# Steps between the matmuls of a one-core attention and feed-forward block: features inside the last queries' matmuls, output weights and row steps with free steps between, memory steps one by one as their buffers need

## The chip, the core and the metric

The kernel runs on one core of a Trainium2 chip, in one launch. The metric is the device time of that launch in microseconds, lower is better. The engines of the core run side by side, each through its own queue in order: TensorE (PE in the profile) multiplies, VectorE (DVE), ScalarE (ACT) and GpSimd (POOL) work element by element, and SyncE (SP) issues most of the transfers; ScalarE issues some too. An instruction that waits holds up everything behind it on its engine.

## The reference, cut to what matters

```
x: 2048 rows of 512;  mod = silu(c) @ w_mod  ->  sa, ca, ga, sb, cb, gb
h  = layernorm(x) * (1 + ca) + sa
q, k, v = h @ wq, h @ wk, h @ wv          # 32 heads of 16, 4 segments of 512 rows
for each segment s:
    a_dot = softmax(q k^T / 4 + causal mask) v          # inside the segment
    a_mem = phi(q) M / (phi(q) z + 1e-6)                # phi(t) = t + 1 if t > 0 else exp(t)
    o     = g * a_mem + (1 - g) * a_dot                 # g = sigmoid(beta), one for each head
    M, z += phi(k)^T v, sum of phi(k)
x  = x + ga * (o @ wo)
h  = layernorm(x) * (1 + cb) + sb
x  = x + gb * (((h @ w_gate) * (h @ w_up)) @ w_down)    # hidden size 1376
```

Data are float32. The kernel keeps float32 accuracy with products of high and low halves: a matrix `a` becomes `aH` (a copy in a shorter format, made by ScalarE) and `aL = a - aH` (made by VectorE or GpSimd), and a product takes three matmuls, H x H, L x H and H x L.

## The kernel before

**Attention loop.** The heads are worked through in 32 units `u` of four heads each: unit `u` belongs to segment `u // 8` and group `u // 2 % 4` of eight heads. The main loop runs over `v` from -2 to 32, with five slots each. In slot `i` of turn `v` TensorE computes logits for the row maxima of a unit one or two ahead (`q_step`: tiles `q`, reduced by VectorE into `nm`), does what `fill` gives it, and then the logits of unit `v` (`k_step`: tile `k`, turned by ScalarE into `pt` with one Exp, masked by GpSimd). Once per turn 16 products with the values (`av_step`, tile `tb`) are put in. There is one buffer for `k`, so the `k_step` of a slot waits until ScalarE has read the one before. The maxima of a unit go through a transpose (`ntp`, `nt`) and by DMA into two extra rows of its queries (`n_step`). I call "row v.i" what TensorE does from the `k_step` of slot i in turn v to the next `k_step`.

**Fill.** All other work of the block is cut into steps by two generators, `fill_a` (attention: row statistics and features `a_ln`, projections `a_kq` and `a_v`, memory steps `a_mem`, conditioning `a_mod`) and `fill_b` (output projection `wo_mm`, second layer norm `lnC`, first steps of the feed-forward part). A step yields its cost on TensorE; `fill` takes steps until the slot's credit is used up. `yield 0.0` costs nothing, `yield False` ends the slot's filling, `yield None` means that nothing can be done yet. `weave(a, b, at)` runs `a` and puts one step of `b` behind each place of `a` that `at` names.

**Features.** `a_ln(s + 1)` makes, for the next segment, row statistics (four steps), the reciprocal deviation (ScalarE, then five small operations on GpSimd), four scalings of rows on VectorE, and then for each of four column blocks d a transpose (`atp`), a scaled copy (`ahf`, ScalarE), `ahH` (ScalarE) and `ahL` (GpSimd). The first projection of the next segment, `kps{s+1}_0`, reads `ahH` and `ahL` of all four blocks, one after the other.

**Memory steps.** `a_mem(s, g)` transposes phi(k) (`mp`, copied to `pkr`), multiplies phi(q) with the memory in two halves (`up`, copied to `us`) and updates the memory (`mz`); one PSUM buffer (`sm`) serves them all. `memq` holds the waiting generators; `drain` runs all of them before the phi of a query projection is allocated. phi tiles rotate through three buffers.

**After the loop** comes the feed-forward part: 22 weight preparations (`prep`, each loading `w_gate` and `w_up` columns by four DMAs and splitting them into halves `AH`, `AL`), products `g`, and the down projection `acc`.

**What sets the order.** A scheduler places the instructions of each engine; matmuls are chained in program order, and `pin` ties an instruction behind the last matmul issued before it. An instruction that is not pinned can be placed earlier. Eight semaphores serve all DMAs in turn, so a DMA can be issued only once the DMA eight before it has landed.

## Time and profile before

| what | value |
|---|---|
| time, median of 3 runs | 881.3 us (879.98 to 881.94) |
| the profiled execution, its own time | 881.91 us |
| its span, first to last instruction | 879.8 us |
| mean granted TensorE clock | 0.992 |
| busy: TensorE, VectorE, ScalarE, GpSimd | 832.8, 650.6, 472.5, 424.1 us |
| attention loop, first to last `k_step` | 59.1 to 516.1 us of the span |

A line of the timeline gives start, length, engine, source line, operation, tiles (out<-in, buffer numbers left out), shape and count, and in brackets how long the engine had been idle before it and what ended that. L90 is the helper through which every matmul goes, L40 one through which VectorE's operations go, so the tile names tell the place.

### The profile page before, as it was taken

The numbers are of one execution on the slowest core, as the hardware profiler recorded it, in microseconds if no ns is written. First come the engines' busy times: TensorE is split into PE (matmuls) and PEld (weight loads), VectorE is DVE, ScalarE is ACT, GpSimd is POOL, SyncE is SP. The second block draws the span as 40 slices with busy tenths as digits, with TensorE's granted clock in tenths as the row PEclk, the third lists the DMA queues.
The fourth block names the chain that finished last, engine by engine and source line by source line (L and its number), as shares of the span: only waits on it lengthen the run. The fifth ranks groups of instructions, "written<-read, shape, count | busy, mean of one in ns | idle before, by whom it ended". The sixth has DMA issues, their size and how long they took to land.

```text
span 879.8 us, 14406 instructions
## 1 busy us (share of the span) xinstructions
PE 832.8 (95%) x4824; PEld 583.0 (66%) x4824; DVE 650.6 (74%) x1728; ACT 472.5 (54%) x740; POOL 424.1 (48%) x564
## 2 busy tenths in 40 slices
PE   8998999989999989999978899999999999999998
PEld 5765565555565656655644567788778888887886
DVE  7697677986778868788888759898784856666532
ACT  3757667777677766777554664333363523333321
POOL 4545546546455665486352533987200846550000
PEclk9999899999999999999999999999999999999999
DMA  7774456665648665677695552543414232212032
GB/s 236 225 235 159 146 160 201 214 209 174 207 142 252 199 190 157 220 234 239 209 285 177 160 180 97 176 146 105 163 30 127 87 120 64 56 55 93 0 118 96
DMA packets 112667, 139.46 MB, mean 159 GB/s; under 512 B 20112, under 2 KB 71312, under 8 KB 112592
## 3 DMA queue, kind: packets, MB, share of 16 engines
q1 hardware_dynamic: 106368, 130.91, 48.7%
q10 hardware_dynamic: 6224, 7.62, 2.4%
q8 instruction: 38, 0.62, 0.3%
q14 instruction: 37, 0.30, 0.1%
HBM read 87.48 MB, written 50.76 MB: 157 GB/s over the span
## 4 chain that ended last, share of the span: by engine, by line
PE 66%; DVE 13%; DMA 8%; ACT 5%; POOL 4%; issue 3%; ACTq 1%; SPq 0%; POOLq 0%; DVEq 0%
PE g L90 23%; PE acc L90 14%; PE tb L90 5%; DVE q L40 5%; PE k L90 5%; PE q L90 5%; PE vps L90 4%; PE kps L90 3%; PE qps L90 2%; ACT pt L330 2%; DMA xr<-in_x_dram 2%; PE wops L90 2%; POOL ahL L223 1%; DVE x L40 1%; DVE nm L40 1%
## 5 line engine op out<-in xcount | busy, mean ns | idle before, releaser
L40 DVE CUSTOM_DVE_ANT_0 q<-q,cmask 128x384 f32<-128x384 f32 (+3 forms) x512 | 246.7, 508 | 66.4 <-PE q L90 56.4
L330 ACT ACTIVATE pt<-k 128x1024 f32<-128x1024 f32 x160 | 163.8, 1024 | 68.7 <-PE k L90 47.3
L333 POOL TENSOR_SCALAR_AFFINE_SELECT pt<-pt 128x256 f32<-128x256 f32 (+1 forms) x224 | 105.4, 484 | 174.3 <-ACT pt L330 173.9
L90 PE MATMUL q<-kst,qst 96*128 96x384 bf16 (+3 forms) x512 | 102.1, 301 | 11.7 <-DVE nm L40 10.4
L90 PE MATMUL k<-qst,kst 98*128 98x384 bf16 (+3 forms) x512 | 97.9, 303 | 11.6 <-ACT pt L330 10.7
L448 POOL TENSOR_TENSOR w<-w 128x256 f32<-128x256 f32 (+1 forms) x84 | 72.0, 869 | 55.7 <-DMA w<-in_w_up_dram 38.2
L443 POOL TENSOR_TENSOR AL<-w,AH 128x512 fp32r<-128x512 f32 (+1 forms) x42 | 58.2, 1388 | 48.0 <-ACT AH L439 46.8
L90 PE MATMUL tb<-pt,v 128*32 128x512 f32 (+3 forms) x1024 | 76.2, 438 | 0.2 <-POOL pt L333 0.2
L90 PEld LDWEIGHTS <-kst 98*128 98x128 bf16 x512 | 38.8, 99 | 56.6 <-issue 48.4
L40 DVE DVE_READ_ACCUMULATOR2_ANT nm<- 128x1 f32 x512 | 72.3, 141 | 0.0
L90 PEld LDWEIGHTS <-qst 96*128 96x128 bf16 x512 | 43.6, 98 | 39.1 <-issue 14.4
L439 ACT ACTIVATE AH<-w 128x512 fp32r<-128x512 f32 (+3 forms) x88 | 46.8, 565 | 33.6 <-POOL w L448 20.5
L1453 DVE TENSOR_TENSOR mL<-mid,mH 128x512 fp32r<-128x512 f32 (+1 forms) x44 | 32.9, 751 | 41.4 <-ACT mH L1452 39.4
L90 PE MATMUL acc<-DH,mL 128*128 128x512 f32 x144 | 56.6, 393 | 0.9 <-DVE mL L1453 0.9
L90 PE MATMUL acc<-DH,mH 128*128 128x512 f32 x144 | 57.2, 397 | 0.0
L90 PE MATMUL acc<-DL,mH 128*128 128x512 f32 x144 | 56.5, 393 | 0.0
L90 PEld LDWEIGHTS tb<-pt,v 128*32 128x32 f32 x1024 | 28.7, 110 | 39.5 <-issue 35.9
L1452 ACT ACTIVATE mH<-mid 128x512 fp32r<-128x512 f32 (+1 forms) x44 | 27.1, 627 | 51.7 <-PE acc L90 50.1
L1245 ACT ACTIVATE p<-g 128x512 f32<-128x512 f32 (+1 forms) x22 | 13.1, 597 | 73.2 <-PE g L90 73.1
L443 DVE TENSOR_TENSOR AL<-w,AH 128x512 fp32r<-128x512 f32 (+3 forms) x44 | 29.2, 671 | 19.1 <-ACT AH L439 18.2
L359 ACT ACTIVATE tsb<-tb 128x512 f32<-128x512 f32 x32 | 19.1, 596 | 35.0 <-PE tb L90 33.4
L90 PE MATMUL g<-chH,AH 128*128 128x512 f32 (+1 forms) x88 | 34.8, 395 | 0.7 <-ACT p L1245 0.7
(286 smaller groups left out, 2060.1 us busy)
## 6 DMA issues: line engine op xcount, KB each, us to landing
kst<-kd SPq DMA_DIRECT2D x32, 384.0 KB
qst<-qd SPq DMA_DIRECT2D x32, 384.0 KB
td<-tsb ACTq DMA_DIRECT2D x28, 256.0 KB
wm<-in_w_mod_dram SPq DMA_DIRECT2D x24, 256.0 KB
kd<-k SPq DMA_DIRECT2D x16, 384.0 KB
qd<-q SPq DMA_DIRECT2D x16, 384.0 KB
w<-in_w_gate_dram SPq DMA_DIRECT2D x40, 128.0 KB
w<-in_w_up_dram SPq DMA_DIRECT2D x40, 128.0 KB
```

Of the source, the lines that this page charges most:

```text
L40: i = getattr(self.eng, name)(*a, **k)
L90: return pe(nc.tensor.matmul(*a, **k))
L223: nc.gpsimd.tensor_sub(lo, h, hi.bitcast(F32))
L330: lpt[0] = act.activation(pt, kp, AF.Exp, scale=0.25)
L333: sels[u, i] = nc.gpsimd.affine_select(w, w, pattern=[[0, w.shape[1]], [1, P]], compare_op=ALU.is_ge, fill=0.0, base=0, channel_multiplier=-1)
L359: act.activation(tsbs[u], tbs.pop(u), AF.Copy)
L439: i = act.activation(hi[sl], w[sl], AF.Copy)
L443: i = eng.tensor_sub(lo[sl], w[sl], hi[sl].bitcast(F32))
L448: i = ce.tensor_tensor(w[:, o, :, 0:n], w[:, x, :, 0:n], w[:, y, :, 0:n], op=op)
L1245: lcp[0] = act.activation(r["p1"], ps, AF.Copy)
L1452: pin(act.activation(mH[0:n], md[0:n], AF.Copy))
L1453: vec.tensor_sub(mL[0:n], md[0:n], mH[0:n].bitcast(F32))
```

## The change

1. Features: the slot-ending steps between column blocks now stand only in the second layer norm, and `a_ln` is woven so that the four blocks of the next segment come out inside the last query projection (`qps{s}_3`) instead of behind it.
2. Memory steps: `drain` is gone. Before a phi tile is allocated, memory steps run only while the user of the tile three before it is not done (for the last segment: all, as before). The VectorE operation that ends phi (`later`) waits one more slot unless someone asks for it.
3. Output weights: all four tiles of `wo` are loaded at once into the buffers of the rows, and scaling, high half and low half of a tile stand in three different steps; the two first residual tiles take the buffers that the weights had. In `wo_op` the high half is pinned too, and the low half is made one step later.
4. Row steps of the second layer norm, and the first weight preparation (`prep(0, ...)`), take other places between the products of the output projection: the preparation moves from beside `wo_mm(1)` to beside `wo_mm(2)`.
5. DMAs: the two row transfers of `n_step` become one (32 fewer on ScalarE's queue), the four loads of a weight preparation three (22 fewer on SyncE's).

```diff
@@ -226,7 +226,7 @@
             if kept_h is not None:
                 kept_h.append(h)
             yield 0.45
-            if not first and d % 2 == 1:
+            if pfx == "c" and d % 2 == 1:
                 yield False
         return hH, hL
 
@@ -306,8 +306,7 @@
         TP(tp, nms.pop(u).rearrange("p a b -> p (a b)"), identb)
-        for i in range(2):
-            nc.scalar.dma_start(Q[96 + i:97 + i].rearrange("p h (q t) -> p (h q) t", t=P), nt[16 * i:16 * i + 16])
+        nc.scalar.dma_start(Q[96:98].rearrange("p h (q t) -> p (h q) t", t=P), nt)
 
     def k_step(u, i):
 
@@ -428,8 +427,9 @@
 
         f0, n = ft[i]
         w = rpool.tile([P, 8, 2, P], F32, tag="W", name=f"w{key}", bufs=rb)
-        for src, k0, j in ((w_gate, 0, 0), (w_gate, 2, 1), (w_up, 0, 7), (w_up, 2, 2)):
-            pin(nc.sync.dma_start(w[:, j, :, 0:n], src.rearrange("(k p) f -> p k f", p=P)[:, k0:k0 + 2, f0:f0 + n]))
+        wk = w.rearrange("p j k f -> p (j k) f")
+        for src, k0, nk, j in ((w_gate, 0, 4, 0), (w_up, 0, 2, 14), (w_up, 2, 2, 4)):
+            pin(nc.sync.dma_start(wk[:, j:j + nk, 0:n], src.rearrange("(k p) f -> p k f", p=P)[:, k0:k0 + nk, f0:f0 + n]))
         yield 0.0
         hi = pool.tile([P, 7, 2, P], F32R, tag="AH", name=f"AH{key}", bufs=nb)
         lo = pool.tile([P, 7, 2, P], F32R, tag="AL", name=f"AL{key}", bufs=nb)
@@ -474,6 +474,11 @@
 
     def wo_op(s, pb, rw, us, gs=range(NG)):
 
+        prev = ()
+
+        def sub(oL, a, oH):
+            pin(vec.tensor_sub(oL, a, oH.bitcast(F32)))
+
@@ -489,11 +494,14 @@
             else:
                 a = rw[g]
                 oL = a.bitcast(F32R)
-            act.activation(oH, a, AF.Copy)
+            pin(act.activation(oH, a, AF.Copy))
             us.append((oH, oL))
+            if prev:
+                sub(*prev)
+            prev = oL, a, oH
             yield 0.0
-            pin(vec.tensor_sub(oL, a, oH.bitcast(F32)))
-            yield 0.0
+        sub(*prev)
+        yield 0.0
 
     def both(a, b):
         while True:
@@ -509,7 +517,7 @@
-            xr = pb.tile([P, D], F32, tag=tag, name=f"xr{s}_{t}", bufs=4)
+            xr = pb.tile([P, D], F32, tag=tag, name=f"xr{s}_{t}", bufs=2 if pb is wpool else 4)
@@ -737,10 +745,14 @@
     done = set()
     later = []
 
-    def flush():
-
-        while later:
-            later.pop(0)()
+    def flush(now=()):
+
+        for x in later[:]:
+            if x[1] > 0 or x[2] in now:
+                later.remove(x)
+                x[0]()
+            else:
+                x[1] += 1
 
     phs = {}
 
@@ -792,8 +804,9 @@
             if phi:
                 if fast:
                     yield 0.0
-                if nm == "q" and g > 0:
-                    yield from drain()
+                phlog.append((s, g, nm))
+                while memq and (s == NSEG - 1 and g > 0 or len(phlog) > 3 and phlog[-4] not in phdone):
+                    yield mem_step() or 0.0
                 e = pa.tile([P, L], F32, tag="ph", name=f"ph{nm}{s}_{g}", bufs=3)
                 rl = pa.tile([P, L], F32, tag="rl", name=f"rl{nm}{s}_{g}", bufs=1)
 
@@ -811,14 +824,15 @@
                 give()
                 rest()
             if phi:
-                later.append(lambda: pin(vec.scalar_tensor_tensor(e, e, 1.0, rl, op0=ALU.min, op1=ALU.add)))
+                later.append([lambda: pin(vec.scalar_tensor_tensor(e, e, 1.0, rl, op0=ALU.min, op1=ALU.add)), 0, nm])
                 if fast:
-                    flush()
+                    flush("kq")
         nkq[s, g] = nkq.get((s, g), 0) + 1
         if nkq[s, g] == 2:
             done.add((s, g))
 
     memq, memt, nkq = [], [], {}
+    phlog, phdone = [], set()
 
     def mem_step():
         for mq in ((memt, memq) if len(memt) > 1 else (memq, memt)):
@@ -830,24 +844,19 @@
                 if mq is memq and not memq:
                     return None
 
-    def drain():
-        while memq:
-            w = mem_step()
-            if w is not None:
-                yield w
-
     def a_mem(s, g):
 
         ph = phs.pop((s, g))
         yield 0.0
         give()
-        flush()
+        flush("k")
         if s < NSEG - 1:
             mp = pst((P, 512), "sm", f"mp{s}_{g}")
             for t in range(4):
                 TP(mp[:, t * P:(t + 1) * P], ph["k"][:, t * P:(t + 1) * P], ident)
             pkr = pa.tile([P, 4, P], F32, tag="pkr", name=f"pkr{s}_{g}", bufs=1)
             act.activation(pkr.rearrange("p a b -> p (a b)"), mp, AF.Copy)
+            phdone.add((s, g, "k"))
             yield 0.5
         if s > 0:
             while len(memt) > 1:
@@ -856,6 +865,7 @@
                     memt.pop(0)
                 else:
                     yield w
+            flush("kq")
             den = pa.tile([P, 4, HG], F32, tag="den", name=f"den{s}_{g}", bufs=2)
             mem = pa.tile([P, 4, HG, DH], F32, tag="mem", name=f"mem{s}_{g}", bufs=2)
             ups = pa.tile([P, 4, HG, VS], F32, tag="ups", name=f"us{s}_{g}", bufs=1)
@@ -865,6 +875,8 @@
                     MM(up[:, t % 2].rearrange("p h e -> p (h e)"), ph["q"][:, t * P:(t + 1) * P],
                        MZ[g].rearrange("p h e -> p (h e)"), start=True, stop=True)
                 act.activation(ups[:, 2 * i:2 * i + 2], up, AF.Copy)
+                if i == 1:
+                    phdone.add((s, g, "q"))
                 yield 0.5
             pin(vec.tensor_scalar_add(den, ups[:, :, :, DH], 1e-6))
             vec.reciprocal(den, den)
@@ -921,31 +933,24 @@
 
     def wo_weights():
 
...
+        B["wo"] = hs, ls = [], []
+        raw = []
+        for k in range(KT):
+            raw.append(pa.tile([P, D], F32, tag="x", name=f"wor{k}", bufs=4))
             pin(nc.sync.dma_start(raw[k], wo[k * P:(k + 1) * P, :]))
-
...
+        yield 0.0
+        yield 0.0
+        for k in range(KT + 2):
+            if k < KT:
+                pin(nc.gpsimd.tensor_mul(raw[k], raw[k], gab))
+            if 1 <= k <= KT:
+                hs.append(wpool.tile([P, D], F32R, tag="eight", name=f"woH{k - 1}", bufs=8))
+                pin(act.activation(hs[-1], raw[k - 1], AF.Copy))
+            if k > 1:
+                ls.append(wpool.tile([P, D], F32R, tag="eight", name=f"woL{k - 2}", bufs=8))
+                i = (vec if k % 2 else nc.gpsimd).tensor_sub(ls[-1], raw[k - 2], hs[k - 2].bitcast(F32))
+                pin(i)
+            yield 0.0
 
     def open_b():
         close(papool)
@@ -974,18 +979,19 @@
                     if g == 2:
                         xts[s + 1] = xload(s + 1)
                         lns = a_ln(s + 1)
-                        Q = weave(Q, lns, (0, 1, 2, 3) if s > 0 else (2, 3))
+                        K = weave(K, lns, (2, 3) if s > 0 else (3,))
+                        Q = weave(Q, lns, (0, 1, 2) if s > 0 else (0, 1, 2, 3))
                     else:
-                        K = weave(K, lns, (0, 2) if s > 0 else (0, 1, 2, 3))
-                        Q = weave(Q, lns, (0, 1, 2))
+                        K = weave(K, lns, (1, 1, 2, 2))
+                        Q = weave(Q, lns, (0, 1, 2, 3))
                 if g == 1 and 0 < s < 3:
                     acc = mod_acc(r)
                     K, Q = weave(K, acc, (0, 2)), weave(Q, acc, (0, 2))
                 if s == NSEG - 1 and g == 1:
-                    xr0 = xr_load(0, pa, (0, 1), "x")
+                    xr0 = xr_load(0, wpool, (0, 1), "wor")
                     ready = chain(wo_weights(), wo_op(0, None, B["orl"], us[0]))
                 if s == NSEG - 1 and 0 < g < NG - 1:
-                    K, Q = weave(K, ready, (0, 1, 2, 3)), weave(Q, ready, (0, 1, 2, 3))
+                    K, Q = weave(K, ready, (0, 2)), weave(Q, ready, (0, 2) if g == 1 else (0, 2, 3))
                 if s == NSEG - 1 and g == NG - 1:
                     yield from weave(Q, ready, (0, 1, 2, 3))
                     memq.append(a_mem(s, g))
@@ -1020,17 +1026,20 @@
         rest = wo_mm(0, us[0], xr_load(0, pb, (2, 3)), (2, 3))
         o1 = wo_load(1, pb)
         pr = prep(0, "0_0", bc, 1, pb, 1)
+        op = wo_op(1, pb, o1, us[1])
+        yield from weave(rest, op, (4, 5, 6, 7))
         next(pr)
-        yield from weave(rest, wo_op(1, pb, o1, us[1]), (3, 4, 4, 5, 5, 6, 6, 7))
         B["o0"] = True
         lg = lnC(0, pb, bc, pb, "x1", 4)
-        yield from weave(wo_mm(1, us[1], xr_load(1, pb)), chain(pr, islice(lg, 10)), (0, 1, 2, 3, 4, 6, 7, 8, 9, 10, 11, 12, 13, 14))
+        yield from weave(wo_mm(1, us[1], xr_load(1, pb)), chain(op, islice(lg, 10)),
+                         (0, 1, 4, 5, 6, 7, 8, 11, 12, 13, 14))
         while "o2" not in B:
             yield None
-        yield from weave(kept_as("nxt", lg), wo_op(2, pb, B["o2"], us[2]), (0, 0, 1, 1, 2, 2, 3, 3))
+        yield from weave(kept_as("nxt", lg), wo_op(2, pb, B["o2"], us[2]), (0, 1, 2, 3, 3))
         B["orl_free"] = True
         lg = lnC(1, pb, bc, pb, "x1", 4)
-        yield from weave(wo_mm(2, us[2], xr_load(2, pb)), lg, (0, 1, 2, 3, 4, 5, 6, 7, 8, 9))
+        rest = weave(wo_mm(2, us[2], xr_load(2, pb)), lg, (0, 3, 4, 5, 6, 7, 10, 11, 12, 13))
+        yield from weave(rest, pr, (1, 8, 9, 14))
         B["hf"] = yield from lg
 
     def kept_as(nm, g):
```

The places at which instructions stand otherwise, word for word from the built programs. TensorE, end of row 5.4: `qps1_1` is a query projection, `mz1_0` the memory update of group 0, `mc3` the column sums of the conditioning rows `wm3_0`, which GpSimd adds up; `k6_0` is the next slot's `k_step`. Before:

```order
L90 MATMUL up1_0_1_1864<-MZ0_220,phq1_0_1350 128x136 x2
L90 MATMUL qps1_1_1817<-ahH1_3_1163,wqH1_496 128x512
L90 MATMUL qps1_1_1817<-ahH1_3_1163,wqL1_497 128x512
L90 MATMUL qps1_1_1817<-ahL1_3_1164,wqH1_496 128x512
L90 MATMUL mz1_0_1880<-v1_0_208,pkr1_0_1762 128x136
L90 MATMUL mz1_0_1880<-v1_1_209,pkr1_0_1762 128x136
L90 MATMUL mz1_0_1880<-v1_2_210,pkr1_0_1762 128x136
L90 MATMUL mz1_0_1880<-v1_3_211,pkr1_0_1762 128x136
L90 LDWEIGHTS kst2_226
L90 MATMUL k6_0_1890<-qst2_230,kst2_226 128x512
```

Now:

```order
L90 MATMUL up1_0_1_1857<-MZ0_220,phq1_0_1345 128x136 x2
L90 MATMUL qps1_1_1810<-ahH1_3_1155,wqH1_496 128x512
L90 MATMUL qps1_1_1810<-ahH1_3_1155,wqL1_497 128x512
L90 MATMUL qps1_1_1810<-ahL1_3_1156,wqH1_496 128x512
L90 MATMUL mc3_1881<-ones_72,wm3_0_1675 128x1 x4
L90 LDWEIGHTS kst2_226
L90 MATMUL k6_0_1887<-qst2_230,kst2_226 128x512
```

`mc3` stands directly behind `qps1_1`, and `mz1_0` has gone to the row after `k6_0`.

ScalarE, turns 26 and 27: `oH1_x` are the high halves of loaded attention rows `orl1_x`, `AH0_0` those of the first weight preparation, `td26` and `qst0` DMAs. Before:

```order
L330 ACTIVATE pt26_4_5728<-k26_4_5723 128x1024
L492 ACTIVATE oH1_0_5741<-orl1_0_5655 128x512
L492 ACTIVATE oH1_1_5750<-orl1_1_5657 128x512
L330 ACTIVATE pt27_0_5758<-k27_0_5755 128x1024
L492 ACTIVATE oH1_2_5813<-orl1_2_5659 128x512
L492 ACTIVATE oH1_3_5819<-orl1_3_5661 128x512
L359 ACTIVATE tsb26_5788<-tb26_5771 128x512
L330 ACTIVATE pt27_1_5796<-k27_1_5793 128x1024
L361 DMA td26_169<-tsb26_5788 128x512
L439 ACTIVATE AH0_0_5865<-w0_0_5663 128x512
L330 ACTIVATE pt27_2_5829<-k27_2_5824 128x1024
L310 DMA qst0_228<-nt28_5835 1x16x128 x2
```

Now:

```order
L497 ACTIVATE oH1_0_5714<-orl1_0_5628 128x512
L329 ACTIVATE pt26_4_5695<-k26_4_5690 128x1024
L329 ACTIVATE pt27_0_5722<-k27_0_5719 128x1024
L497 ACTIVATE oH1_1_5776<-orl1_1_5630 128x512
L497 ACTIVATE oH1_2_5782<-orl1_2_5632 128x512
L358 ACTIVATE tsb26_5752<-tb26_5735 128x512
L329 ACTIVATE pt27_1_5760<-k27_1_5757 128x1024
L360 DMA td26_169<-tsb26_5752 128x512
L497 ACTIVATE oH1_3_5813<-orl1_3_5634 128x512
L329 ACTIVATE pt27_2_5793<-k27_2_5788 128x1024
L309 DMA qst0_228<-nt28_5799 2x16x128
L329 ACTIVATE pt27_3_5843<-k27_3_5838 128x1024
```

The first half stands one exponential earlier, the others one apart, the two transfers of `nt28` are one, and the weight copies are gone from here.

ScalarE, turn 9: `ahf2_d` and `ahH2_d` are the features of segment 2. Before:

```order
L899 ACTIVATE mTs1_1_2535<-mT1_1_2530 128x512
L205 ACTIVATE ahf2_0_2542<-atp2_0_2543,modc_83 128x512
L205 ACTIVATE ahf2_1_2553<-atp2_1_2554,modc_83 128x512
L330 ACTIVATE pt9_2_2569<-k9_2_2564 128x1024
L222 ACTIVATE ahH2_0_2549<-ahf2_0_2542 128x512
L310 DMA qst2_230<-nt10_2575 1x16x128 x2
L205 ACTIVATE ahf2_2_2592<-atp2_2_2593,modc_83 128x512
L222 ACTIVATE ahH2_1_2560<-ahf2_1_2553 128x512
L330 ACTIVATE pt9_3_2619<-k9_3_2614 128x1024
L222 ACTIVATE ahH2_2_2599<-ahf2_2_2592 128x512
L205 ACTIVATE ahf2_3_2603<-atp2_3_2604,modc_83 128x512
L222 ACTIVATE ahH2_3_2610<-ahf2_3_2603 128x512
```

Now, where the same features stand (turn 8):

```order
L205 ACTIVATE ahf2_0_2348<-atp2_0_2349,modc_83 128x512
L329 ACTIVATE pt8_2_2367<-k8_2_2362 128x1024
L222 ACTIVATE ahH2_0_2355<-ahf2_0_2348 128x512
L309 DMA qst1_229<-nt9_2373 2x16x128
L911 ACTIVATE mTs1_0_2391<-mT1_0_2386 128x512
L205 ACTIVATE ahf2_1_2393<-atp2_1_2394,modc_83 128x512
L329 ACTIVATE pt8_3_2409<-k8_3_2404 128x1024
L222 ACTIVATE ahH2_1_2400<-ahf2_1_2393 128x512
L205 ACTIVATE ahf2_2_2424<-atp2_2_2425,modc_83 128x512
```

The features have moved up by about one turn, among the copies of `kps1_3` and `qps1_3`.

22 lines of the change are left out of this document (1 added, 21 removed).

## The prediction

> **What bounds the kernel now.** I read the page first, then the busy time by stage, then the chain of waits of TensorE alone, and at last single lines of the timeline around its longest idle places.
>
> The page's first part gives each engine's busy time:
>
> ```profile
> PE 832.8 (95%) x4824; PEld 583.0 (66%) x4824; DVE 650.6 (74%) x1728; ACT 472.5 (54%) x740; POOL 424.1 (48%) x564
> ```
>
> TensorE is the bound, with 47 us of the 879.8 us span idle. Where those lie shows the table by stage. Its columns: stretch, length, busy time of PE, PEld, DVE, ACT and POOL, granted clock, DMA share, GB/s. The stretches are the attention loop without its last part, the part in which the last queries are projected and the first output projections run beside the attention, the loop's end, and the feed-forward part.
>
> ```profile
> 59.10:441.80 382.70, 359.62 (x2550) 222.44 (x2550) 304.46 (x1071) 268.80 (x396) 217.66 (x316) 0.99 0.63 195
> 441.80:492.20 50.40, 40.21 (x272) 23.94 (x271) 40.24 (x132) 26.02 (x37) 20.95 (x37) 0.97 0.69 215
> 492.20:516.10 23.90, 22.25 (x155) 13.37 (x152) 15.18 (x42) 13.10 (x17) 13.08 (x23) 1.00 0.54 155
> 516.10:879.80 363.70, 357.60 (x1597) 286.09 (x1596) 246.19 (x363) 134.36 (x244) 145.17 (x144) 1.00 0.33 101
> ```
>
> After 516.10 TensorE is busy for 357.60 of 363.70 us, and its order there is unchanged: nothing to win. Of the 47 us, 23.1 lie in the first row and 10.2 in the second, a stretch of only 50.4 us. TensorE's waits in these two (total us, times, longest), first 59.1 to 441.8:
>
> ```profile
> PE q L90 <- DVE nm L40: 6.4, 16, 0.5
> PE k L90 <- ACT pt L330: 4.6, 7, 1.5
> PE kps L90 <- POOL ahL L223: 4.3, 7, 1.3
> PE mz L90 <- ACT us L867: 2.9, 5, 0.9
> PE up L90 <- ACT us L867: 2.3, 2, 1.3
> PE up L90 <- ACT pkr L850: 1.0, 1, 1.0
> PE kps L90 <- ACT ahf L205: 0.7, 1, 0.7
> PE kps L90 <- ACT ahH L222: 0.3, 1, 0.3
> ```
>
> then 441.8 to 492.2:
>
> ```profile
> PE k L90 <- ACT pt L330: 6.1, 4, 2.3
> PE q L90 <- DVE nm L40: 1.9, 4, 0.6
> PE ctp L93 <- DVE x L40: 1.4, 1, 1.4
> PE k L90 <- DMA qst<-nt: 0.4, 1, 0.4
> PE ctp L93 <- DVE xr L40: 0.3, 1, 0.3
> ```
>
> Three groups are what the change touches: `kps` waiting for features (4.3 + 0.7 + 0.3 = 5.3 us), the memory steps waiting for ScalarE's copies (2.9 + 2.3 + 1.0 = 6.2 us), and the second list, 10.1 us. The 6.4 us of `q` behind the maxima `nm` is VectorE's pace, and the change leaves it.
>
> **The change part by part.** All sums stand against the profiled execution's 881.91 us, 0.6 above the median of the three runs, 881.3.
>
> *Features.* The waits at the three segment changes (84 to 92, then 197 to 206, then 308 to 323 us):
>
> ```profile
> PE kps L90 <- POOL ahL L223: 1.5, 2, 1.3
> PE kps L90 <- ACT ahf L205: 0.7, 1, 0.7
> ...
> PE kps L90 <- POOL ahL L223: 1.9, 3, 1.0
> ...
> PE k L90 <- ACT pt L330: 2.0, 2, 1.5
> PE kps L90 <- POOL ahL L223: 1.0, 2, 0.7
> PE kps L90 <- ACT ahH L222: 0.3, 1, 0.3
> ```
>
> The feature steps move up by about a turn, so `kps2_0` and `kps3_0` find all blocks made: 1.9 and 1.0 + 0.3 us go, and with ScalarE's features out of the way of `pt` the 2.0 us too. For segment 1 the fourth block of `kps1_0` still stands behind an exponential and its mask; of 1.5 + 0.7 I leave 1.1. In the third change two users move close behind their copies (`atp3_1` behind `ahf3_0`, `mp2_2` behind `mTs2_0`); I charge 0.9, the mean of 0.7 and 1.0 from such waits above. Sum: 1.1 + 1.9 + (3.3 - 0.9) = 5.4 us gained. The steps' new cover is the products of `qps{s}_3`; without it they would cost the same 5.3 us one turn earlier, so between 0 and 6.3.
>
> *Memory steps.* `mz` and `up` are now spread one to a slot, each a slot behind its copy: 6.2 us go, but the pair `up3_2` keeps both halves in one row (1.3, the longest of `up`). Gain 4.9 us; bounds 0 (the waits only move) and 6.2.
>
> *A new wait.* With `mz1_0` gone from the end of row 5.4, the column sums `mc3` follow `qps1_1` directly. In the timeline (start, length, ..., idle before) around it on TensorE, and then GpSimd's last addition of `wm3_0`:
>
> ```profile
> 144.68 0.40 PE L90 MATMUL qps<-ahL,wqH 128*128 128x512 f32 x1
> 145.57 1.19 PE L90 MATMUL mz<-v,pkr 128*128 128x136 f32 x8 [0.49 <-ACT us L867]
> ...
> 146.24 1.26 POOL L620 TENSOR_TENSOR wm<-wm,wm 128x512 f32<-128x512 f32 x1
> ```
>
> TensorE is free at 145.08 (144.68 + 0.40), and the addition ends at 147.50: 2.4 us of new idle time, with `k6_0` queued behind it, and so ScalarE's `pt6_0` and the mask. It falls to nothing if GpSimd's two additions start a slot earlier, which the order does not show; I take 2.4.
>
> *Turn 23.* Copies of the first attention rows now meet phi's operations of segment 3 on ScalarE there. One such copy lasts 0.63 us (row 444.79 below); between 0 and three copies, 1.9. I take 0.5: one copy, mostly covered.
>
> *Last queries.* The longest idle places of the second list, with what ScalarE and SyncE did:
>
> ```profile
> 435.91 0.34 SPq L527 DMA_DIRECT2D x1d<-xr  x1
> ...
> 440.78 1.84 SPq L471 DMA_DIRECT2D orl<-od  x4
> 444.79 0.63 ACT L492 ACTIVATE oH<-orl 128x512 fp32r<-128x512 f32 x1 [3.36 <-DMA orl<-od]
> 447.65 0.59 PE L90 MATMUL k<-qst,kst 98*128 98x512 bf16 x2 [2.28 <-ACT pt L330]
> ...
> 454.31 1.90 ACTq L310 DMA_DIRECT2D qst<-nt  x2
> 456.31 1.02 ACT L330 ACTIVATE pt<-k 128x1024 f32<-128x1024 f32 x1 [4.50 <-DVE nm L40]
> 457.38 0.60 PE L90 MATMUL k<-qst,kst 98*128 98x256 bf16 x4 [2.26 <-ACT pt L330]
> ...
> 486.35 0.33 PE L93 MATMUL ctp<-ident,x 128*128 128x128 f32 x1 [1.36 <-DVE x L40]
> ```
>
> At 444.79 ScalarE sat 3.36 us at a copy whose rows had been asked for only at 440.78, and the exponential behind it was late: 2.28 us on TensorE. Now the first residual rows have buffers of their own, so SyncE can issue those loads right behind 435.91, some 4 us earlier, and the copies are pinned one apart. At 454.31 two small transfers held ScalarE's queue for 1.90 us and the exponential came 2.26 us late; one transfer is left. The weight copies are out of these turns. From 10.1 us I keep 1.9 (`nm`) and 1.0 (a load that the row statistics may meet): 7.2. But VectorE is busy for 40.24 us here and would fill 93% of the 43.2 us that are left; for its collisions I take 1.4 more, the size of the `ctp` wait. Gain 5.8 us; bounds 0 and 8.2.
>
> *Transfers.* 32 fewer issues on ScalarE's queue are counted at row 454.31, the only place where one shows among TensorE's long waits; elsewhere I take 0. In the feed-forward part 22 fewer issues on SyncE's queue lie beside a full TensorE: 0. A loss here is the fourth rival.
>
> *Clock.* Two stretches of the loop were granted half the clock. The table's rows for them, each behind the 3.4 us ahead of it, and a third such place that stayed at full clock:
>
> ```profile
> 84.20:87.60 3.40, 1.67 (x8) 0.86 (x5) 1.86 (x8) 3.40 (x7) 3.40 (x3) 1.00 0.91 306
> 87.60:94.40 6.80, 6.40 (x21) 3.09 (x25) 1.30 (x6) 2.94 (x6) 3.77 (x6) 0.50 0.60 187
> 483.60:487.00 3.40, 1.77 (x12) 1.11 (x9) 3.33 (x14) 1.65 (x3) 0.76 (x2) 0.99 0.07 22
> 487.00:490.40 3.40, 3.40 (x14) 2.49 (x15) 1.51 (x4) 3.23 (x5) 1.55 (x2) 0.50 0.71 205
> 446.00:449.40 3.40, 1.75 (x8) 1.23 (x8) 3.16 (x14) 3.35 (x6) 0.41 (x1) 1.00 1.11 298
> ```
>
> Both follow a stretch in which TensorE was busy for about half the time (1.67 and 1.77 of 3.40), with no single gap over 1.36 us in it (row 486.35, and 1.3 for `kps`). The third, at 1.75, did not trip, so half busy is the edge. Features fill the first of the two and the `ctp` wait's going fills the second. Half of 6.80 and of 3.40 us come back, 3.4 + 1.7 = 5.1; the 2.4 us hole at `mc3` may open a new one, 1.7. Net gain 3.4; bounds -1.7 and 5.1. The Trainium skill, "TensorE: Matmul & The Clock Gate", section "Why this matters for your kernels", asks only that gaps between bursts stay under about 3 us, one whole idle window being what brings back the slow clock. By that rule none of these gaps costs clock and filling them wins none: the term would be 0 in place of 3.4. The trace speaks against it here, half clock standing behind gaps of at most 1.36 us.
>
> *Sum:* -5.4 - 4.9 + 2.4 + 0.5 - 5.8 - 3.4 = -16.6 us. What is late next: the mean wait of `q` behind `nm` in the first list is 6.4 / 16 = 0.4 us. Some 24 waits go; I let nine of them be followed by one of these, +4.0 (rounded up), as TensorE then runs closer to VectorE. Net -12.6: 869.3 for the profiled execution, 868.7 by the median; I say 869.0.
>
> **Rivals.**
>
> *Half clock stays* (0.17). The pace of the attention, not the single wait, may hold TensorE near half busy in the same stretches. For it: the third place above shows that 1.75 busy decides nothing. Against it: each period followed a named wait that goes. Time: 881.9 - 13.2 + 4.0, less 0.6, is 872.1; it is also what the skill's rule gives.
>
> *Half of each gap is refilled* (0.16): VectorE at 304.46 of 382.70 us and ScalarE at 268.80 become late where TensorE comes earlier, and the half clock stays. For it: 16 waits behind `nm` now. Against: no engine but TensorE is above 80% in the first stretch. (5.4 + 4.9 + 5.8) / 2 = 8.1 gained, 2.9 lost: 881.9 - 5.2, less 0.6, is 876.1.
>
> *Slower: the transfers' turns* (0.14). Eight semaphores serve all transfers in turn; with 54 fewer of them, each `nt` transfer now follows another one eight before it, which can be a large load that SyncE issued late. ScalarE then stands at the issue with the exponential queued behind it, and `k_step` behind that. Price: 2.26 us each, as at row 457.38. It decides from 12.6 / 2.26 = 5.6, that is six of the 32 units; at eight, 18.1 us are lost: 887.4, less 0.6, is 886.8. For it: 454.31 shows the mechanism. Against: it shows it once among 32.
>
> *Nothing comes back* (0.06): the waits move to the next users, 881.3.
>
> **How the numbers follow.** The forecast has 0.47, and its own range is 865 to 872. The low end of the whole range takes the forecast without successors (865.3), without the `mc3` wait (-2.4), and with the two amounts kept in the last queries (1.0 and 1.4) gained: 860.5. The high end takes in the refilled case with its 2.9 us of new waits once more: 879.0. Left out are the slower case and most of the case without change, 0.14 + 0.06. A difference of 0.2% (1.8 us) is about what a measurement of this kernel can tell from none. Faster by more: 0.47 + 0.17 + 0.16 = 0.80; same 0.06; slower 0.14.
>
> **What would show it.** Right: no `kps` behind `ahL` at the second and third segment change; `mz` and `up` with at most 2 us of waits together; ScalarE without an idle place over 2 us at 440 to 460; full clock where 87.6 and 487.0 stood; and a wait of `mc` behind `wm` of about 2.4 us. Wrong: half clock at other places, more than 12 us of `q` behind `nm` in the loop, or `pt` behind an `nt` transfer in six turns or more.

## The result and the profile after

| | before | after |
|---|---|---|
| median of 20 runs each | 881.26 us (877.43 to 887.16) | 876.2 us (873.13 to 882.98) |
| ratio, 95% interval | 1 | 0.9946 (0.9926 to 0.9966) |
| the profiled execution, its span | 881.91, 879.8 us | 873.19, 871.1 us |
| mean granted clock, profiled | 0.992 | 0.995 |

The change is faster by 5.1 us, not by the 12.3 of the forecast, and the time lies inside the range that was given. The profiled execution of after is one of its fastest: 8.7 us below that of before, where the medians are 5.1 apart. Both numbers are needed below. The executions of the experiments that ran at a much lower granted clock (0.749 or 0.556; the profiles of `p_feat`, `h_hole` and `g_dve` were among them) stand in none of the times, and no line of these three profiles is read.

The page's first line after:

```profile
PE 828.9 (95%) x4823; PEld 581.2 (67%) x4824; DVE 658.9 (76%) x1728; ACT 474.5 (54%) x740; POOL 423.3 (49%) x564
```

The table by stage, cut at the same rows of the program (27.0 begins at 438.99 now, 442.03 before):

```profile
0.00:57.90 57.90, 52.48 (x256) 35.97 (x257) 44.58 (x119) 30.88 (x48) 28.28 (x48) 1.00 0.80 241
57.90:438.90 381.00, 358.51 (x2551) 222.92 (x2551) 307.68 (x1078) 270.33 (x397) 215.66 (x315) 0.99 0.64 199
438.90:483.40 44.50, 38.24 (x269) 22.58 (x269) 37.94 (x130) 23.63 (x33) 15.19 (x29) 1.00 0.66 206
483.40:506.80 23.40, 21.95 (x154) 13.42 (x154) 16.05 (x38) 14.64 (x21) 18.67 (x29) 1.00 0.53 161
506.80:871.10 364.30, 357.73 (x1597) 286.36 (x1596) 252.67 (x364) 135.05 (x244) 145.52 (x145) 1.00 0.32 100
```

By stage: -1.2 us (59.1 to 57.9), -1.7 (382.7 to 381.0), -5.9 (50.4 to 44.5), -0.5, +0.6. The cut at 438.9 lies at the end of a new wait of 1.66 us ahead of row 27.0: its time is in the first stretch, but the lists of waits below count it in the second. Cut ahead of that wait, the two stretches give -3.3 and -4.3. The long first stretch of the attention, in which the forecast saw most of its gain, gave 1.7 us (3.3 without that wait). TensorE's waits there:

```profile
PE q L90 <- DVE nm L40: 10.1, 19, 1.6
PE k L90 <- ACT pt L329: 4.1, 10, 0.7
PE mc L90 <- POOL wm L628: 2.4, 1, 2.4
PE kps L90 <- POOL ahL L223: 0.9, 1, 0.9
PE mp L93 <- ACT mTs L911: 0.8, 1, 0.8
PE up L90 <- ACT us L877: 0.8, 1, 0.8
PE kps L90 <- ACT ahH L222: 0.4, 1, 0.4
PE mz L90 <- ACT us L877: 0.4, 1, 0.4
PE mz L90 <- ACT pkr L858: 0.4, 1, 0.4
PE atp L93 <- ACT ahf L205: 0.2, 1, 0.2
```

and in the last queries (438.9 to 483.4):

```profile
PE k L90 <- ACT pt L329: 4.5, 3, 1.7
PE ctp L93 <- DVE x L40: 1.3, 1, 1.3
PE q L90 <- DVE nm L40: 0.7, 2, 0.4
PE wops L90 <- DVE orl L40: 0.4, 1, 0.4
PE ctp L93 <- DVE xr L40: 0.3, 1, 0.3
```

In the first list the waits at which the change aimed fell from 13.5 us (5.3 features, 6.2 memory steps, 2.0 of `k`) to 3.9 (0.9 + 0.4 + 0.2 + 0.8, and 0.8 + 0.4 + 0.4). But 2.4 us are new at `mc`, `q` behind `nm` grew from 6.4 to 10.1, and the rest of `k` behind `pt` from 2.6 to 4.1: of 9.6 us, 7.6 came back as other waits.

### The profile page after: what moved, and what is told of

Its sections match the earlier page's. It is cut to its first block, busy times and chain, and to the rows that moved or that the text cites. A ratio compares the mean times of both kernels' runs of the same rounds, so it can differ in the third digit from the quotient of the medians.

```text
span 871.1 us, 14342 instructions
## 1 busy us (share of the span) xinstructions
PE 828.9 (95%) x4823; PEld 581.2 (67%) x4824; DVE 658.9 (76%) x1728; ACT 474.5 (54%) x740; POOL 423.3 (49%) x564
## 4 chain that ended last, share of the span: by engine, by line
PE 66%; DVE 13%; ACT 7%; DMA 5%; POOL 3%; issue 3%; SPq 0%; ACTq 0%; POOLq 0%; DVEq 0%
PE g L90 23%; PE acc L90 14%; PE tb L90 5%; PE k L90 5%; PE q L90 5%; DVE q L40 4%; PE vps L90 4%; PE kps L90 2%; ACT pt L329 2%; PE wops L90 2%; PE qps L90 2%; DVE x L40 2%; DMA x1d<-xr 1%; DMA x<-in_x_dram 1%; PE mz L90 1%
## 5 line engine op out<-in xcount | busy, mean ns | idle before, releaser
L448 POOL TENSOR_TENSOR w<-w 128x256 f32<-128x256 f32 (+1 forms) x84 | 73.9, 893 | 56.0 <-DVE t L1205 37.9
L443 POOL TENSOR_TENSOR AL<-w,AH 128x512 fp32r<-128x512 f32 (+1 forms) x42 | 56.4, 1345 | 48.4 <-ACT AH L439 48.3
L443 DVE TENSOR_TENSOR AL<-w,AH 128x512 fp32r<-128x512 f32 (+3 forms) x44 | 35.2, 803 | 9.2 <-ACT AH L439 9.0
```

What stands on the lines that cost most here:

```text
L443: i = eng.tensor_sub(lo[sl], w[sl], hi[sl].bitcast(F32))
L448: i = ce.tensor_tensor(w[:, o, :, 0:n], w[:, x, :, 0:n], w[:, y, :, 0:n], op=op)
```

## Experiments

Times of different kernels are compared by their ratio to the kernel before, run on the same chip beside them. "Clock" is the mean granted clock over the executions; "idle" is the sum of TensorE's waits in the attention loop of the one profile (in the row of `p_feat`, of its second profile, `p_feat_look`). The last column is the mean time. The kernels ran on different chips, and the mean of the kernel before was 881.4 to 882.4 us on them, so a conclusion is drawn from the ratios; a difference of two of them is uncertain by about 0.3% (2.6 us).

| kernel | ratio (95%) | clock | idle us | mean us |
|---|---|---|---|---|
| before | 1 | 0.9901 | 34.2 | 881.7 |
| after | 0.9946 (0.9926 to 0.9966) | 0.9910 | 29.6 | 877.0 |
| p_feat: part 1 alone | 1.0040 (1.0019 to 1.0061) | 0.9855 | 34.1 | 885.9 |
| p_mem: part 2 alone | 1.0025 (1.0006 to 1.0044) | 0.9856 | 36.2 | 884.9 |
| p_last: parts 3, 4 alone | 0.9969 (0.9947 to 0.9991) | 0.9916 | 32.0 | 880.5 |
| p_dma: part 5 alone | 0.9971 (0.9952 to 0.9989) | 0.9898 | 30.6 | 879.7 |
| p_nt: its first half alone | 0.9964 (0.9942 to 0.9985) | 0.9902 | 30.3 | 878.5 |
| p_fm: parts 1 and 2 | 1.0027 (1.0009 to 1.0045) | 0.9866 | 32.2 | 883.6 |
| fm_hole: the same, `mc3` later | 0.9984 (0.9960 to 1.0008) | 0.9874 | 34.2 | 881.0 |
| no_last: after without 3, 4 | 1.0036 (1.0014 to 1.0058) | 0.9857 | 34.5 | 884.5 |
| no_dma: after without 5 | 0.9993 (0.9972 to 1.0014) | 0.9882 | 31.3 | 880.9 |
| h_hole: after, `mc3` later | 0.9911 (0.9885 to 0.9937) | 0.9924 | | 873.5 |
| c_fill: after, hole filled | 0.9914 (0.9889 to 0.9939) | 0.9943 | 31.9 | 874.5 |
| s_spread: after, scalings apart | 0.9952 (0.9931 to 0.9973) | 0.9921 | 34.5 | 877.3 |
| o_late: after, high halves later | 0.9957 (0.9935 to 0.9979) | 0.9886 | 30.1 | 877.8 |
| g_dve: after, low halves on VectorE | 0.9950 (0.9933 to 0.9968) | 0.9924 | | 876.8 |
| best | 0.9892 (0.9865 to 0.9918) | 0.9948 | 29.3 | 871.7 |

My theory once the result was known ("moved"): the named waits went, and other waits took their place. The rival ("clock"): the waits stay gone, and half clock elsewhere takes the time back.

### One part at a time

Each kernel is the one before with the lines of the named part of the diff and no others.

> The kernel before with part 1 alone (features inside the last query projections). Theory 'moved': the features' waits of TensorE fall from 5.3 us to about 1.3, but the four row scalings of a segment now stand together on VectorE and the maxima wait behind them, so q behind nm grows by about 2 us in the loop; net about -2 us, 879. Theory 'clock': the waits go and stay gone (-5 us in the profile's idle time), and what is missing in the time is half clock elsewhere: mean granted clock no better than 0.992. The forecast's own term: -5.4 and the first half-clock stretch gone, 873 to 876.

> The kernel before with part 2 alone (memory steps as their buffers need). Both theories: mz and up behind ScalarE fall from 6.2 us to about 1.6, and mc behind wm appears with 2.4 us at the end of row 5.4; net -2.2 of idle time, so 879 (-2). The forecast's own terms: -4.9 + 2.4, the same size. Theory 'clock': a half-clock stretch behind the new hole in most executions, mean granted clock lower than before by 0.002, time then unchanged.

> The kernel before with parts 3 and 4 alone (output weights, row steps, first weight preparation). Theory 'moved': the two waits of k behind pt with 2.3 us each become one of about 1.7 at the first high half, which stands one exponential earlier while its rows come only some 2 us earlier, and one of about 1.5 later; the list of 10.1 us falls by about 3 and the loop's last turns gain a wait of tb of about 1 us: net -2, 879. The forecast's own term: -5.8, 875.

> The kernel before with part 5 alone (one transfer for two in each turn, three for four in each weight preparation). The forecast's own term without the stall at the second small transfer: 0 to -2 us, 879 to 881. The rival of the transfers' turns: pt or k behind a transfer in six turns or more, +5 us or more. 'Moved' expects waits of about 1.5 us at one or two other places on ScalarE's queue: 880 to 881.

The parts that the forecast priced highest cost time when they stand alone: part 1 +0.40%, part 2 +0.25%, worse than either theory expected. Parts 3, 4 and part 5 gain 0.3% each. In both that lose, the clock is lower as well (0.9855 and 0.9856 against 0.9901). Part 1 once more, for its waits, and parts 1 and 2 together:

> Part 1 alone once more, for its waits: kps behind features at most 1.5 us in all; if 'each other's room' holds, waits of memory steps (up, mz, mp) or of k behind pt of 3 us or more in rows 8.1 to 8.4 and 16.1 to 16.4, where the drained memory steps and the features now meet.

> The kernel before with parts 1 and 2 together (features and memory steps), nothing else. Alone they cost time: 885.9 and 884.9 (means; before 882.1), +3.8 and +2.8. Theory 'each other's room': the features need the slots that the drained memory steps leave, and the memory steps the slots that the features leave, so the two together gain: 880 or less (-2). Theory 'sum': the two costs add up to +6 to +7, 888, and the whole change's gain must come from parts 3 to 5 interacting with them.

TensorE's two largest waits in the loop, before and then in that one execution of part 1 (879.22 us):

```profile
PE k L90 <- ACT pt L330: 10.7, 11, 2.3
PE q L90 <- DVE nm L40: 9.7, 22, 0.9
...
PE q L90 <- DVE nm L40: 14.9, 21, 2.6
PE k L90 <- ACT pt L330: 8.1, 11, 1.8
```

The feature waits were gone but for 1.7 us of `kps`; `k` behind `pt` fell by 2.6, but `q` behind `nm` grew by 5.2, so the sum stayed (34.1 for 34.2). The memory steps in rows 8.1 to 8.4 cost 1.3 us, not 3: "each other's room" is not shown, and the two together still cost 0.27%. That is "sum" in sign, at about a third of its size.

### Each part left out

> The changed kernel with parts 3 and 4 undone (features, memory steps and transfers stay). The forecast gave these parts -5.8; alone on the kernel before they gave -1.3 (880.5 against 881.9, means). If parts add up: 877.0 + 1.3 = 878.3. If they are worth more beside the others, because their row work and the features share VectorE: 880 or more.

> The changed kernel with part 5 undone (two small transfers in each turn, four loads in each weight preparation). The forecast gave it 0; alone it gave -2.1 (879.7). If parts add up: 879.1. If the transfers only mattered at the stall that parts 3 and 4 remove anyway: 877.

Left out, parts 3 and 4 are worth 0.90% (1.0036 to 0.9946, 7.9 us), alone 0.31% (2.7); part 5 is worth 0.47% (4.1), alone 0.29% (2.6). For parts 3 and 4 the difference is clear of the noise, for part 5 it isn't. What parts 3 and 4 mend is not in the last queries alone. Without them, VectorE in row 22.0 (a line each of ScalarE, VectorE and TensorE; `no_last`):

```profile
372.09 0.63 ACT L939 ACTIVATE woH<-wor 128x512 fp32r<-128x512 f32 x1 [0.15 <-POOL wor L935]
372.76 0.97 DVE L40 TENSOR_TENSOR woL<-wor,woH 128x512 fp32r<-128x512 f32 x1 [2.91 <-ACT woH L939]
374.70 0.38 PE L90 MATMUL q<-kst,qst 96*128 96x256 bf16 x2 [2.06 <-DVE nm L40]
```

VectorE stands 2.91 us at the low half of an output weight, because high and low half are issued in one step and ScalarE's copy waits for GpSimd's scaling; the maxima are queued behind, and TensorE loses 2.06 us (2.6 in the row). The same place with parts 1 and 2 alone (`p_fm`), and in the kernel before:

```profile
376.66 1.50 DVE L40 TENSOR_TENSOR woL<-wor,woH 128x512 fp32r<-128x512 f32 x1 [3.80 <-ACT woH L939]
```

```profile
375.64 1.33 DVE L40 TENSOR_TENSOR woL<-wor,woH 128x512 fp32r<-128x512 f32 x1
```

All four profiles that have part 1 and lack part 3 show this wait in row 22.0 (2.6 to 2.9 us of TensorE's time: `p_feat_look`, `p_fm`, `fm_hole`, `no_last`); before and after have none there. It costs more than its length: in all four, half clock begins within 4.1 us of the start of TensorE's wait (at 374.0, 379.9, 370.7 and 376.7 us), and in none of the other eleven profiles at this row. Three steps for scaling, high and low half take the wait away. That is one named piece of what parts 3 and 4 are worth beside parts 1 and 2; no run mends this wait by itself, so how much of the 7.9 us it is stays open. The whole against its parts' sum tells less: -0.54% against -0.31 - 0.29 + 0.27 = -0.33%, a difference within the noise.

### The transfers

```diff
-        for i in range(2):
-            nc.scalar.dma_start(Q[96 + i:97 + i]..., nt[16 * i:16 * i + 16])
+        nc.scalar.dma_start(Q[96:98]..., nt)
```

> The kernel before with the first half of part 5 alone, one transfer for two in each turn. If ScalarE's queue is what part 5 relieves, all of its -2.1 is here: 879.7 to 880. If it is the order in which transfers take their turns, which the loads of the feed-forward part cannot change before their own time: the same. If the gain is in the weight loads: 881.9.

As far as intervals of 0.2% on each tell, all of part 5 is in this half (ratio 0.9964; part 5 whole 0.9971). The stall of 1.90 us at 454.31 is one single issue now (`p_nt`):

```profile
453.57 0.62 ACTq L309 DMA_DIRECT2D qst<-nt  x1
454.29 1.03 ACT L329 ACTIVATE pt<-k 128x1024 f32<-128x1024 f32 x1 [1.98 <-POOL w L447]
```

and TensorE's wait in row 27.3 (2.26 before) is gone; in the profile of `p_dma` 1.15 us of it are left. The forecast had counted that row inside the last queries and put 0 on the rest. A gain of 2.6 to 3.2 us alone is not clearly more than this one row.

### The hole at mc3, and the clock

```diff
                 if g == 1 and 0 < s < 3:
+                    if s == 1:
+                        yield False
                     yield from a_mod(2 * s + 1, r[0])
```

> The changed kernel with the column sums mc3 one slot later, so that TensorE does not stand at GpSimd's additions at the end of row 5.4. Theory 'moved': the wait of 2.4 us goes, half of it is met again at the next maxima or exponential: -1 to -2.4 us against the changed kernel's 876.2, 874 to 875. Theory 'clock': more than the wait comes back, 2.4 and half of a 3.4 us stretch in half of the executions: -3 to -4, 872 to 873.

> Parts 1 and 2 with mc3 one slot later, so without the hole at the end of row 5.4 (parts 1 and 2 alone: 883.6, mean). Theory 'the hole and its clock': -2.4 for the wait and -0.9 for one half-clock stretch, 880.3, and the mean granted clock higher by 0.002. If the wait is met again at the next exponential: 882 to 883.

Taking the hole away gives 0.35% (3.1 us) in the changed kernel and 0.43% (3.8 us) beside parts 1 and 2 alone. Both are gains, but neither is told from the 2.4 us of the wait itself, and the clock beside parts 1 and 2 rose by 0.0008 and not by 0.002. Whether the clock has a share shows a kernel that leaves the wait and only keeps TensorE busy in it (the tile `ps` is made a whole bank wide for that):

```diff
+        if nm == "mc3":
+            x = hcur[0][0][0]
+            for _ in range(9):
+                MM(ps, x[:, 0:P], x, start=True, stop=True)
```

> The changed kernel with nine extra products of 128x512 (their result is overwritten) put into the hole ahead of mc3: TensorE still reaches mc3's real work only when GpSimd is done, but it isn't idle. Theory 'clock': no half clock behind the hole, row 6.0 (which took 5.97 us, half clock) lasts about 4.3 us, mean clock higher by 0.001 to 0.002, time -1 to -2 us: 874 to 875. If the hole doesn't matter for the clock: 876 within 1 us, and half clock as often as in the changed kernel.

The place in the changed kernel, TensorE's rows and then two stretches of the table by stage:

```profile
141.29 0.40 PE L90 MATMUL qps<-ahL,wqH 128*128 128x512 f32 x1
144.12 1.05 PE L90 MATMUL mc<-ones,wm 128*128 128x1 f32 x8 [2.43 <-POOL wm L628]
146.00 4.05 PE L90 MATMUL tb<-pt,v 128*32 128x512 f32 x32
...
142.60:146.10 3.50, 1.98 (x18) 1.50 (x22) 0.72 (x3) 1.98 (x5) 3.18 (x3) 1.00 0.97 303
146.10:149.50 3.40, 3.40 (x28) 1.29 (x32) 2.24 (x10) 1.25 (x2) 2.49 (x3) 0.50 0.73 257
```

and with the hole filled (`c_fill`):

```profile
142.32 2.23 PE L90 MATMUL mc<-ahH 128*128 128x512 f32 x9
144.97 1.05 PE L90 MATMUL mc<-ones,wm 128*128 128x1 f32 x8 [0.42 <-POOL wm L628]
146.85 2.36 PE L90 MATMUL tb<-pt,v 128*32 128x512 f32 x32
```

`mc` is reached no earlier (from the last `qps`, 2.83 us there, 2.88 here), but the 32 products behind it take 2.36 us in place of 4.05: half clock is gone. The mean clock rises from 0.9910 to 0.9943, and the ratio falls by 0.32% (2.8 us), which is about as large as its uncertainty. For this place "clock" is right in the trace; its price in time is not sharply measured. Seven profiles have the idle hole, and all seven show half clock within 4 us behind it; in seven without it, and in `c_fill`, none does. The Trainium skill, "TensorE: Matmul & The Clock Gate", section "Why this matters for your kernels", asks for gaps under about 3 us; here a gap of 2.43 us was enough. Nor is it this place alone: in the attention loop of the fifteen profiles TensorE has 14 single waits of 2.37 us or more, and half clock begins within 4 us of the end of each; the two longest of before, 2.28 and 2.26 us, have none.

Elsewhere half clock comes and goes. A stretch that begins between 486 and 493 us stands in five of the fifteen profiles (before, `p_mem`, `p_fm`, `fm_hole`, `no_dma`); one at 87 to 94 in all five that lack part 1, and in one of ten that have it. So part 1 does fill that place. The price of half clock seems smaller than I had it: over 295 executions, compared within each kernel, each microsecond of (1 - clock) x time goes with 0.52 us of time (correlation 0.75), so a stretch of 3.4 us would cost about 0.9 us, not 1.7. That is what goes together in these executions and not a test: by this price the clock of `c_fill` would give 1.5 us, and it gained 2.8, uncertain as those are.

### Three repairs that did not pay alone

The scalings of segment 2 stand together on VectorE, and `q` behind them (after):

```profile
174.89 3.94 DVE L40 TENSOR_SCALAR x<-x,amv,ay 128x512 f32<-128x512 f32 x4
...
179.82 0.38 PE L90 MATMUL q<-kst,qst 96*128 96x512 bf16 x1 [1.38 <-DVE nm L40]
```

```diff
-                        K = weave(K, lns, (1, 1, 2, 2))
+                        K = weave(K, lns, (0, 1, 2, 3))
```

> The changed kernel with the four row scalings one behind each product group of the last key projection in place of two behind each of two. Theory 'moved': the waits of q behind nm in row 8.1 (1.4 + 0.5 us) and row 16.0 (0.5) fall to under 0.6 together: -1 to -2 us, 874 to 875. If the pace of VectorE sets it and not the bunch: no change, 876.

No change. Between 170 and 190 us, where row 8.1 stands, there is no wait for `nm` any more, but the last scaling is now too late for the transpose:

```profile
PE atp L93 <- DVE x L40: 1.8, 1, 1.8
```

TensorE loses 1.8 us there in place of 2.2 (1.9 in row 8.1). That fits VectorE's load and not the bunch as what sets it.

```diff
-        yield from weave(rest, op, (4, 5, 6, 7))
+        yield from weave(rest, op, (5, 6, 7, 7))
```

> The changed kernel with the high halves of the second segment's attention rows one step later, so that the first stands behind the exponential of row 26.4 and not ahead of it. Theory 'moved': the wait of 1.66 us in row 26.4 goes; the products of turn 27 come closer to their halves (0.4 us wait there before, up to 1 now): -0.5 to -1.5 us, 875. If the exponential is late for another reason: no change, 876.

No change (0.9957 against 0.9946). The wait in row 26.4 falls from 1.66 to 0.30 us, and the products of turn 27 then wait 1.6 us for their low half: the halves' own lateness only changes its victim.

```diff
-                i = (vec if k % 2 else nc.gpsimd).tensor_sub(ls[-1], raw[k - 2], hs[k - 2].bitcast(F32))
+                i = vec.tensor_sub(ls[-1], raw[k - 2], hs[k - 2].bitcast(F32))
```

> The changed kernel with all four low halves of the output weights made by VectorE in place of two by GpSimd. In two of the other runs one VectorE operation of row 22.4 (phq, 0.7 us elsewhere) lasted 4.0 us, while GpSimd worked without a gap, and the maxima of row 23.0 came 2.9 us late. Theory 'GpSimd's stream keeps VectorE out': with two operations of 1.3 us taken from that stream the long phq is gone (under 2 us) and row 23.0 waits under 1 us; -1 to -2 us against 876.2. Theory 'VectorE is just full there': two more operations of 0.7 us make it later, +0 to +1 us.

No change either (0.9950 against 0.9946). So the edit doesn't pay; what became of `phq` and of row 23.0 in it is not known, and in the profile of after, where this edit is not made, `phq` was short as well (0.77 us).

### Both kernels beaten

`best` is `h_hole` with the low halves on VectorE and this:

```diff
-        yield from weave(rest, pr, (1, 8, 9, 14))
+        yield from weave(rest, pr, (1, 10, 11, 14))
```

> The changed kernel with mc3 one slot later, the four low halves of the output weights on VectorE, and the second step of the first weight preparation two places later, so that GpSimd's mask of row 31.0 is no longer behind it (wait of tb behind pt 1.4 us there). mc3 alone gave 873.5 (mean). 'Moved' expects another -1.4 for row 31.0 and -1 for row 23.0: 871 to 872. If the freed time is met again at the next exponential: 873 to 874.

Ratio 0.9892 (0.9865 to 0.9918) to before, 0.54% (4.8 us) below the changed kernel. The wait of `tb` behind `pt` in row 31.0 (1.4 us in the changed kernel) is gone and `mc` with it. Row 23.0 still waits 1.42 us, as in the changed kernel. With six executions, what the other two edits add to `h_hole`'s 0.35% is not told.

## Why the prediction was right and wrong

**Features and memory steps, as waits: right.** Forecast -5.4 and -4.9; the waits named fell by 9.6 us in the profile. **As time: wrong, and this is the step that failed.** I let the mean wait of 0.4 us follow nine of 24 waits, 4.0 us in all. In the profile 3.7 (`nm`) and 1.5 (`pt`) came back in the first stretch alone, 5.2 us beside the 2.4 at `mc` that I had priced. By themselves the two parts made the kernel slower by 0.27% (2.4 us), where their terms, with all 4.0 us and the 0.5 of turn 23 counted, come to -3.4. Waits that move explain only a part of this: in `p_fm` the sum of TensorE's waits is 2.0 us below before's. With the rest goes the clock, which I had forecast to rise: 0.9866, against 0.9913 for before on the same chip, is 4.2 us of (1 - clock) x time, about 2.2 us of time at 0.52. New holes make half clock of their own, at `mc` and in row 22.0; I priced one of them, at `mc`.

What I did not look for is what now meets the maxima on VectorE. For the two parts alone it is an operation that stands at another engine with the maxima behind it (`woL`, 2.6 to 2.9 us of TensorE's time), which part 3 takes away again. For the changed kernel it is the row work of the next segment (turns 0, 8 and 16).

**The new wait at `mc`: right** to the size (2.4 forecast, 2.43 measured) and the half clock behind it. I added it to the sum and let it stand; one `yield` mended it.

**Last queries: near in size by luck, reason wrong.** Forecast -5.8, and the stretch fell by 5.9 (4.3 with the wait of 1.66 us counted in it). But the waits in its list fell by 2.9, not by 7.2 less 1.4; most of the rest is the half-clock stretch that the profiled execution of after did not have there (TensorE's busy time fell by 2.0 us). Alone, parts 3 and 4 gave 2.7 us. I had the rows' load 4 us earlier and priced the copy as if it had stayed behind its exponential:

```profile
433.69 0.32 SPq L471 DMA_DIRECT2D orl<-od  x1
437.40 0.63 ACT L497 ACTIVATE oH<-orl 128x512 fp32r<-128x512 f32 x1 [2.59 <-DMA orl<-od]
437.94 1.00 ACT L329 ACTIVATE pt<-k 128x1024 f32<-128x1024 f32 x1
438.99 0.38 PE L90 MATMUL k<-qst,kst 98*128 98x512 bf16 x1 [1.66 <-ACT pt L329]
```

Measured against its row (26.3 begins at 433.07, before at 437.92) the load comes 0.6 us into the row and not 2.9: 2.2 us earlier, and the pinned copy stands one exponential earlier, so the wait of 2.28 became one of 1.66 a row ahead. The moved weight preparation added 1.4 us behind GpSimd in row 31.0, which I had not priced.

**Transfers: too small, by how much is open.** 0 forecast beyond row 27.3, whose 2.26 us stood in the last queries; -2.6 alone in all, -4.1 beside the others. The rival "the transfers' turns" shows at one place and not at six, with ScalarE's `td` issued late and 1.57 us of TensorE's time lost behind it:

```profile
461.28 0.33 ACTq L360 DMA_DIRECT2D td<-tsb  x1
461.71 1.02 ACT L329 ACTIVATE pt<-k 128x1024 f32<-128x1024 f32 x1 [3.80 <-DMA kst<-kd]
```

**Clock: wrong in size.** Forecast -3.4 from two stretches, read as fixed places of the program. One is (87 to 94), one is not, and a stretch may cost 0.9 us and not 1.7. "Half busy is the edge" did not hold either: ahead of the half clock at `mc` TensorE was busy for 1.98 of 3.50 us, more than the 1.75 of 3.40 that stayed at full clock. The mean loss fell from 8.7 to 7.9 us of (1 - clock) x time; at 0.52 that is -0.4 us. Of the signs written ahead, those for TensorE's waits came true; the one for ScalarE did not (idle for 2.36 and 3.80 us before 451.2 and 461.7), and one for being wrong did: half clock at other places, 60.8 and 146.1 us.

**The rivals.** Of what was written ahead, "half of each gap is refilled" (876.1) comes nearest, at 876.2. That it fits to 0.1 us is luck, but its reason is what the waits show: in the first stretch four fifths were refilled, and in the last queries 2.9 of the 7.2 us stayed away. I gave it 0.16 because no engine but TensorE was above 80% busy there; that share is a mean over turns, and the refill stands in turns 0, 8, 15, 16 and 23, where VectorE has the row work of the next segment or the output weights.

## What to carry to other kernels

A wait of the busiest engine that is taken away is worth only the distance to its next wait, and that next wait stands in the queue of the engine that feeds it most often: list what is issued on that engine in the same turns, in order, before a sum is made. Price a new hole twice, for its length and for the clock behind it. An instruction in a shared queue should be issued a step behind the one that it waits for. And where half clock follows a hole that can't be closed, the hole can still be filled: nine products whose result is thrown away took the half clock away here, for about 2.8 us, give or take as much.

## What the runs showed of the hardware

In two profiles one VectorE operation lasted about five times its usual length while GpSimd worked without a break. In `c_fill` (and likewise in `s_spread`, 3.98 us; 0.77 in the same row of after) the row of VectorE, and then GpSimd's:

```profile
381.17 3.96 DVE L40 SCALAR_TENSOR_TENSOR phq<-phq,rlq 128x512 f32<-128x512 f32 x1
...
380.17 1.31 POOL L949 TENSOR_TENSOR wor<-wor,gab 128x512 f32<-128x512 f32 x1
381.42 1.18 POOL L796 TENSOR_TENSOR q<-qr,q 128x512 bf16<-128x512 f32 x1
382.53 0.79 POOL L332 TENSOR_SCALAR_AFFINE_SELECT pt<-pt 128x256 f32<-128x256 f32 x2
383.26 1.32 POOL L955 TENSOR_TENSOR woL<-wor,woH 128x512 fp32r<-128x512 f32 x1
```

It ended at 385.1, half a microsecond behind the last of GpSimd's unbroken row, and cost TensorE 2.9 us in row 23.0, with half clock behind it in both profiles. But GpSimd without a break is not enough. In after it has none in this place either, VectorE's operation is short, and it is GpSimd's next two lines that are long:

```profile
380.56 1.64 POOL L792 TENSOR_TENSOR q<-qr,q 128x512 bf16<-128x512 f32 x1
382.16 1.66 POOL L332 TENSOR_SCALAR_AFFINE_SELECT pt<-pt 128x256 f32<-128x256 f32 x2
```

So it looks as if either engine can hold the other, and which one loses differs between profiles. That is argued from these times; it was not taken apart by a run of its own.
